# Loading keys and queries already turned, and splitting the weights on TensorE one block per slot

## The chip, the cores and the metric

The kernel runs on one core of one Trainium2 chip. The metric is device time in microseconds of one execution. TensorE is called PE (its weight loads PEld), VectorE DVE, ScalarE ACT, GpSimd POOL, and SyncE, which issues all DMAs here, SP.

## The reference

Top-k attention is followed by a channel mix with a gate. Eight batches, eight heads, 576 tokens, head width 64, model width 512, hidden width 1024. For q, k, v of float32:

```python
scores = scale * np.matmul(q, k.transpose(0, 1, 3, 2))      # per batch and head, 576 x 576
kth = np.partition(scores, -32, axis=-1)[..., -32:-31]       # the 32nd largest of each row
scores = np.where(scores >= kth, scores, -1e9)
attn = exp(scores - max);  attn = attn / (sum(attn) + 1e-9)
x = np.matmul(attn, v), heads side by side                   # batch, 576, 512
x_prev = x shifted by one token
xk = mu_k * x + (1 - mu_k) * x_prev;  xr = mu_r * x + (1 - mu_r) * x_prev
out = sigmoid(xr @ w_r) * (np.maximum(xk @ w_k, 0) ** 2 @ w_v)
```

The three weight matrices arrive as float64 and the mix is computed to more than one fp32r product's precision: each operand is split into a coarse part `hi` and a remainder `lo`, both fp32r, and three products are added (`three`).

## The kernel before

**Slots.** The attention works on tiles of 128 query rows by 576 keys, 288 tiles in all: 8 batches x 4 pairs of heads x 9 tiles. Each batch is visited in eight visits: the four head pairs with tiles 0 to 3 (the first 256 tokens), then the pairs in reverse with tiles 4 to 8 (the other 320). The loop over `n` in `pipeline` is a software pipeline. One turn of it, a slot, issues one step of each of several tiles, in the order written out in `ORDER`. Tile n gets its scores on PE (`score`, L237), which ACT copies to SBUF (`keep`, L246). A slot later DVE takes the eight largest of seven pieces (`c0` to `c6`, L270); in the next slot it sorts out the 24 largest (`best`, `drop`, L273, L276), ACT makes a sign against a bound (`count`, L286), POOL multiplies it with the scores (`below`, L289). In the slot after that, DVE finds the last eight candidates (`eighth`, L915, a line at which the trace puts this MAX8), the threshold (L294) and the masked exponentials (`mask`, L300). Then PE turns them (L313), ACT copies them out (`et`, L317), PE weighs the values (L365), and DVE places the result in `xT` (`place`, L371, L376).

**The mix** runs on PE between the attention's steps, in chunks of mostly 256 tokens (`mix_steps`). A piece is one group of matmuls of about 0.7 us (`PIECE`): a gate step, part of a hidden layer, or one eighth of a value tile. A chunk can begin when its tokens are placed. How many pieces go into a slot is decided by a planner when the program is built (`Lanes`, `work`): each slot credits the lane "pe" with `TENSOR`, never above `CAP`, each attention step charges it (`L.use`), and a piece is issued while the credit covers 0.74 of its cost, at most four a slot. In the last 36 slots a piece is charged 0.56. ACT's and POOL's parts of the mix are placed by similar credits of `PACE` a slot. What is left when the attention ends runs in a tail.

**Keys and queries** lie in DRAM as batch, head, token, d, and PE needs d on the partitions. So SP loads staging tiles (`load_keys`, `load_near`, `load_rest`: tiles `kt`, `q_near`, `qr_in`), PE turns them with an identity (`turn`, L206) into a bank of PSUM, and ACT copies them out to `K` (L214), `qs` (L209) and `qr` (L227) one slot later. The step `prep` does this up to four slots ahead of a visit. Keys of a pair stay in one of four buffers (`KEYS`) for both of its visits in a batch. At the start, `prep_first` and `second` do the first pair at once, with two of the copies on DVE (L221). Each turning is charged 0.35 on "pe" and 0.4 on "act"; the copy of the last 64 queries (`turn_rest`) is not charged.

**Weights.** Twenty blocks of 128x512 float64 numbers are loaded (512 KB each) and split on chip in the first slots, one block in each second slot (`weight_steps` yields twice). The two 32-bit words of a number are treated apart: ACT takes the magnitude of the high word (L126), DVE limits it (L130), shifts it and joins it with the sign to a float32 (L131, L132) and takes its power of two (L140). ACT scales the low word (L136) and copies the value to `hi` as fp32r (L148), POOL subtracts `hi`, multiplies the low word by the power and adds (L149 to L151); for w_v POOL halves the value first (L110). All blocks share one staging area, `early`, so the load of a block waits for the use of the one before. The mix waits for the blocks it needs (`g.ready`).

All four PSUM buffers of the pool `psM` are taken in turn by the turned tiles, the turned keys and queries, the shifted weight bits, and the products of the mix.

Of the kernel before, what the change touches and what calls it, by code (L numbers as in the profile page):

```python
# [21 lines left out]
HS = S // 2  # L22
# [3 lines left out]
KB, KP = 3, 96  # L26
# [19 lines left out]
def topk_attention_channel_mix(ctx: ExitStack, tc: tile.TileContext, q, k, v, mu_k, mu_r, w_k, w_v, w_r, out):  # L46
# [7 lines left out]
    make_identity(nc, ident)  # L54
    ranks_i = consts.tile([128, 9], I32, name="ranks_i")
# [37 lines left out]

    def weight_steps(g, L):

        g.early = g.one.tile([128, HP * (1 + S)], F32, name="early", tag="x1")
# [3 lines left out]
        for src, dst, i, c in blocks:  # L100
            weight_block(g, L, src[i * 128:(i + 1) * 128, c:c + 512], *(d[:, i, c:c + 512] for d in dst), half=dst is wv)
            yield
            yield

    def weight_block(g, L, block, hi, lo, half):
        val = g.early[:, 1024:1536].bitcast(U32)
        valf = val.bitcast(F32)

        def halve():
            nc.gpsimd.tensor_scalar(valf, valf, 0.5, 1.0, op0=OP.mult, op1=OP.mult)  # L110

        if block.dtype == F32:
            nc.sync.dma_start(valf, block)
            if half:
                L.at(1, "pool", halve)
            L.at(2, "act", lambda: nc.scalar.activation(hi, valf, AF.Copy))
            L.at(2, "pool", lambda: g.ready.append(nc.gpsimd.tensor_sub(lo, valf, hi.bitcast(F32))))
            return
        st = g.early[:, :1024].bitcast(U32).rearrange("p (c t) -> p c t", t=2)
        nc.sync.dma_start(g.early[:, :1024].bitcast(U32), block.bitcast(U32))  # L120
        low, high = st[:, :, 0], st[:, :, 1]
        W = Env()

        def magnitude():
            W.mag = g.early[:, 1536:2048].bitcast(U32)
            nc.scalar.activation(W.mag.bitcast(F32), high.bitcast(F32), AF.Abs)  # L126

        def shift():
            bits = g.psM.tile([128, 512], U32, name="wbits", tag="pm")
            nc.vector.tensor_scalar(bits.bitcast(F32), W.mag.bitcast(F32), ZERO, None, op0=OP.max)  # L130
            nc.vector.tensor_scalar(bits, bits, 3, 0x3FFFFFFF, op0=OP.logical_shift_left, op1=OP.bitwise_and)  # L131
            nc.vector.scalar_tensor_tensor(val, high, 0xC0000000, bits, op0=OP.bitwise_and, op1=OP.bitwise_or)  # L132

        def fine():
            W.fine = g.one.tile([128, 512], F32, name="wfine", tag="rest")
            nc.scalar.activation(W.fine, low, AF.Copy, scale=2.0 ** -52)  # L136

        def powers():
            W.exp = g.one.tile([128, 512], U32, name="wexp")
            nc.vector.tensor_scalar(W.exp, val, 0xFF800000, None, op0=OP.bitwise_and)  # L140

        L.at(2, "sign", magnitude)
        L.at(2, "act", fine)
        L.at(2, "dve", shift)
        L.at(3, "dve", powers)
        if half:
            L.at(2, "pool", halve)
        L.at(3, "act", lambda: nc.scalar.activation(hi, valf, AF.Copy))  # L148
        L.at(3, "pool", lambda: nc.gpsimd.tensor_sub(valf, valf, hi.bitcast(F32)))  # L149
        L.at(3, "pool", lambda: nc.gpsimd.tensor_mul(W.fine, W.fine, W.exp.bitcast(F32)))  # L150
        L.at(3, "pool", lambda: g.ready.append(nc.gpsimd.tensor_add(lo, valf, W.fine)))  # L151

# [9 lines left out]
    def load_part(g, x, batch, hp, j, tag=None):  # L162
        t = g.one.tile([128, NKC, 2, D], F32, name="kq", tag=tag or f"kq{j}")
        for i in range(2):
            nc.sync.dma_start(t[:, :, i, :], heads(x, batch, hp)[j, :MAIN].rearrange("(p c) d -> p c d", c=NKC))
        return t

    def load_near(g, x, batch, hp, j, c0):

        t = g.one.tile([128, 2, 2, D], F32, name="q_near", tag=f"kq{j}")  # L170
        for i in range(2):
            nc.sync.dma_start(t[:, :, i, :], heads(x, batch, hp)[j, c0 * 128:(c0 + 2) * 128].rearrange("(c p) d -> p c d", p=128))
        return t

    def load_keys(g, batch, hp, j):
        t = g.one.tile([KP, KB, 2, D], F32, name=f"kt{j}")
        for i in range(2):
            nc.sync.dma_start(t[:, :, i, :], heads(k, batch, hp)[j, i * HS:(i + 1) * HS].rearrange("(b p) d -> p b d", p=KP))
        return t

    def load_rest(g, batch, hp):
        t = g.one.tile([128, 1, 2, D], F32, name="qr_in")
        for j in range(2):
            for i in range(2):
                nc.sync.dma_start(t[j * 64:(j + 1) * 64, 0, i, :], heads(q, batch, hp)[j, MAIN:])
        return t
# [9 lines left out]
    def flat(ap):  # L196
        return ap.rearrange("p e d -> p (e d)")

    def new_k(g, P):
        P.K = g.one.tile([128, 2, HS], F32, name="K", tag=f"K{P.home}")  # L200

    def turn(pt, x):

        n = x.shape[0]
        for c in range(x.shape[1]):
            nc.tensor.transpose(pt[:, c * n:(c + 1) * n], flat(x[:, c]), ident[:n, :n])  # L206

    def copy_out(fast):
        return nc.vector.tensor_copy if fast else lambda to, x: nc.scalar.activation(to, x, AF.Copy)  # L209

    def turn_k(g, P, j, L):
        pt = g.psM.tile([128, MAIN], F32, name="pk", tag="pm")[:, :HS]
        turn(pt, P.kt[j])
        L.at(1, "high", lambda: nc.scalar.activation(P.K[:, j], pt, AF.Copy))  # L214

    def turn_q(g, P, j, L, fast=False):
        n = P.qt[j].shape[1] * 128
        pt = g.psM.tile([128, MAIN], F32, name="pq", tag="pm")[:, :n]
        turn(pt, P.qt[j])
        P.qs[j] = g.one.tile([128, n], F32, name=f"qs{j}")  # L220
        L.at(1, "high", lambda: copy_out(fast)(P.qs[j], pt))  # L221

    def turn_rest(g, P, L):
        pt = g.psM.tile([128, MAIN], F32, name="pr", tag="pm")[:, :128]
        turn(pt, P.rest)
        P.qr = g.two.tile([128, 128], F32, name="qr")
        L.at(1, "high", lambda: nc.scalar.activation(P.qr, pt, AF.Copy))  # L227

# [3 lines left out]
    def scores(g, P, i):  # L232
        hs = [slice(e * 64, (e + 1) * 64) for e in range(2)]
        if i < 2 * NKC:
            c, j = divmod(i - P.first, 2)
            for e, h in enumerate(hs):
                nc.tensor.matmul(g.ps[:, e], lhsT=P.qs[j][h, c * 128:(c + 1) * 128], rhs=P.K[h, j], start=True, stop=True)  # L237
        else:
            for j in range(2):
                for e, h in enumerate(hs):  # L240
                    nc.tensor.matmul(g.ps[hs[j], e], lhsT=P.qr[h, hs[j]], rhs=P.K[h, j], start=True, stop=True)
# [125 lines left out]
    def place(U):  # L367
        xT, hp = U.xT, U.P.hp
        if U.u < 2 and U.P.near:
            x = xT[:, hp, 1 + U.u * 256:1 + (U.u + 1) * 256].rearrange("p (u q) -> p u q", u=2)  # L370
            nc.vector.tensor_mul(x, U.pa, U.ri.rearrange("p (u q) -> p u q", u=2))  # L371
        elif U.u < 2:
            x = xT[:, hp, 1:1 + MAIN].rearrange("p (q c) -> p c q", c=NKC)[:, 2 * U.u:2 * U.u + 2, :]
            nc.vector.tensor_mul(x, U.pa, U.ri.rearrange("p (c q) -> p c q", c=2))
# [264 lines left out]
    def prep_all(g, P, batch, hp, L):  # L639
        P.first, P.near, P.home, P.qs = 0, False, 0, {}  # L640
        new_k(g, P)
        P.rest = load_rest(g, batch, hp)
        P.kt, P.qt = [], []
        load_v(g, P, batch, hp)
        for j in range(2):
            P.kt.append(load_keys(g, batch, hp, j))
            turn_k(g, P, j, L)
            P.qt.append(load_part(g, q, batch, hp, j))
            turn_q(g, P, j, L)
        turn_rest(g, P, L)  # L650

    def prep_first(g, P, batch, hp):

        L = Direct()
        new_k(g, P)
        P.kt = [load_keys(g, batch, hp, 0)]
        P.qt = [load_near(g, q, batch, hp, 0, 0)]
        P.kt.append(load_keys(g, batch, hp, 1))
        P.qt.append(load_near(g, q, batch, hp, 1, 0))
        load_v(g, P, batch, hp)  # L660

        def half(j):
            turn_k(g, P, j, L)
            turn_q(g, P, j, L, True)
        half(0)
        return lambda: half(1)
# [370 lines left out]
```

## Time and profile before

| | |
|---|---|
| median of 3 runs | 1322.38 us (1321.73 to 1330.58) |
| profiled execution, its own time | 1321.01 us |
| span in its trace | 1319.2 us |
| mean granted PE clock | 0.950 |
| DMA | 69.48 MB, mean 53 GB/s |

A row of the groups' view names line, engine, operation, tiles (written <- read), shapes and count; then the busy time in all, the mean duration in ns of one, and the idle time of the engine just before, with what ended it. In the view by windows each row begins with the window and its length; each engine's busy us and count follow, then the granted clock of PE, the DMA share and GB/s. In the list of waits an engine and its line wait for another's line, with the us in total, the times, and the longest. Busy PE counts matmuls that overlap at their ends once.

### The profile page before, as it was taken

To read this page: it belongs to the slowest core of one execution; us is meant where nothing else is said; L and a number is where in the kernel's file an instruction comes from. 1 tells how busy PE (TensorE), PEld (TensorE's weight loads), DVE (VectorE), ACT (ScalarE), POOL (GpSimd) and SP (SyncE) were. 2 spreads that over 40 slices of the span, in tenths; PEclk is the share of its full clock that TensorE was granted. 3 is DMA by queue.
4 is the path that set the end of the run, shared out by engine and by line. 5 is a ranking of instruction groups with operands and counts; after the bars stand their busy time and mean duration, and the time that the engine had idled before them with its cause. 6 is when DMAs were issued, how large, how long until landed. Compare 5 with 4: busy or idle time off the path is not lost.

```text
span 1319.2 us, 34927 instructions
## 1 busy us (share of the span) xinstructions
PE 1181.2 (90%) x11157; PEld 939.8 (71%) x11157; DVE 1128.6 (86%) x6388; ACT 1107.9 (84%) x2716; POOL 907.0 (69%) x837
## 2 busy tenths in 40 slices
PE   5756786899989899799989999999999999999997
PEld 3434564676867688577867787878787787778786
DVE  6999988888998999889998999999999898898100
ACT  5778886889998899898989999999999898898431
POOL 3768887668656866786658776778676758677662
PEclk9766888899999999899989999999999999999999
DMA  4232232211321122112221132122212221111000
GB/s 108 81 93 72 75 94 55 51 33 35 75 63 33 34 63 69 37 37 66 54 58 31 37 75 54 42 55 50 62 43 53 51 59 42 46 40 28 13 17 23
DMA packets 204912, 69.48 MB, mean 53 GB/s; under 512 B 197552, under 2 KB 197552, under 8 KB 204720
## 3 DMA queue, kind: packets, MB, share of 16 engines
q1 hardware_dynamic: 204720, 67.16, 20.4%
q8 instruction: 91, 1.49, 0.5%
q14 instruction: 101, 0.83, 0.2%
HBM read 57.68 MB, written 9.44 MB: 51 GB/s over the span
## 4 chain that ended last, share of the span: by engine, by line
PE 56%; DVE 16%; ACT 15%; POOL 9%; issue 2%; SPq 0%; DMA 0%; ACTq 0%; DVEq 0%; POOLq 0%
PE ps L365 10%; PE ps L237 8%; PE ph L424 5%; PE ph L425 4%; PE ph L426 4%; PE pv L424 4%; PE pt L313 4%; PE pv L426 4%; PE pv L425 3%; DVE cand L270 3%; ACT sc L246 3%; ACT sg L286 3%; DVE E L300 3%; POOL sg L289 3%; DVE top L915 2%; PE pz L424 2%
## 5 line engine op out<-in xcount | busy, mean ns | idle before, releaser
L289 POOL TENSOR_TENSOR sg<-sc,sg 128x576 f32<-128x576 f32 x288 | 410.5, 1425 | 283.2 <-ACT sg L286 277.5
L270 DVE MAX8 cand<-sc 128x8 f32<-128x82 f32 (+1 forms) x2016 | 468.3, 233 | 1.4 <-ACT sc L246 0.9
L915 DVE MAX8 top<-sg 128x8 f32<-128x576 f32 x288 | 217.7, 756 | 40.6 <-POOL sg L289 39.0
L246 ACT ACTIVATE sc<-ps 128x576 f32<-128x576 f32 x288 | 188.9, 656 | 71.2 <-PE ps L237 44.1
L286 ACT ACTIVATE sg<-sc,seen 128x576 f32<-128x576 f32 x288 | 224.5, 780 | 16.1 <-DVE seen L281 14.8
L237 PE MATMUL ps<-K,qs 64*128 64x288 f32 x1024 | 206.8, 483 | 32.8 <-DVE xT L371 15.3
L300 DVE SCALAR_TENSOR_TENSOR E<-sc,seen,se 128x576 f32<-128x576 f32 x288 | 231.8, 805 | 0.6 <-DVE cand L270 0.3
L297 ACT ACTIVATE se<-sc,seen 128x576 f32<-128x576 f32 x288 | 218.7, 759 | 3.6 <-DVE E L300 3.5
L317 ACT ACTIVATE et<-pt 128x320 f32<-128x320 f32 x576 | 219.7, 441 | 0.7 <-PE pt L338 0.7
L313 PEld LDWEIGHTS pt<-ident,E 64*128 64x128 f32 x2880 | 140.8, 145 | 103.6 <-issue 17.1
L365 PE MATMUL ps<-et,v_in 128*64 128x128 f32 (+1 forms) x2560 | 176.4, 285 | 28.1 <-ACT sc L246 19.4
L313 PE MATMUL pt<-ident,E 64*128 64x64 f32 x2880 | 151.2, 232 | 34.2 <-DVE E L300 19.6
L365 PEld LDWEIGHTS ps<-et,v_in 128*64 128x64 f32 x2560 | 146.2, 149 | 48.9 <-ACT sc L246 33.3
L424 PE MATMUL ph<-xh,wk 128*128 128x256 f32 (+2 forms) x608 | 178.9, 294 | 0.4 <-ACT qs L209 0.2
L273 DVE MAX8 top<-cand 128x8 f32<-128x56 f32 x864 | 177.2, 205 | 0.1
L425 PE MATMUL ph<-xl,wk 128*128 128x256 f32 (+2 forms) x608 | 170.8, 281 | 0.0
L426 PE MATMUL ph<-xh,wk 128*128 128x256 f32 (+2 forms) x608 | 170.6, 281 | 0.0
L237 PEld LDWEIGHTS ps<-K,qs 64*128 64x128 f32 x1024 | 81.8, 195 | 81.8 <-ACT sc L246 20.8
L425 PE MATMUL pv<-wv,hh 128*128 128x512 f32 (+1 forms) x296 | 118.1, 399 | 10.7 <-POOL wv L151 10.7
L426 PE MATMUL pv<-wv,hl 128*128 128x512 f32 (+1 forms) x296 | 118.8, 401 | 7.9 <-POOL hl L445 7.9
L424 PE MATMUL pv<-wv,hh 128*128 128x512 f32 (+1 forms) x296 | 125.1, 423 | 0.0
L424 PEld LDWEIGHTS ph<-xh,wk 128*128 128x128 f32 x608 | 116.0, 191 | 5.7 <-ACT qs L209 0.4
(91 smaller groups left out, 2474.9 us busy)
## 6 DMA issues: line engine op xcount, KB each, us to landing
q_near<-in_q SPq DMA_DIRECT2D x256, 64.0 KB, 2.1
v_in<-in_v SPq DMA_DIRECT2D x128, 128.0 KB, 2.5
kt<-in_k SPq DMA_DIRECT2D x128, 72.0 KB, 2.2
out<-eb SPq DMA_DIRECT2D x35, 256.0 KB, 2.1
early<-in_moe_w_k SPq DMA_DIRECT2D x8, 512.0 KB, 3.7
early<-in_moe_w_v SPq DMA_DIRECT2D x8, 512.0 KB, 3.4
vr_in<-in_v SPq DMA_DIRECT2D x64, 32.0 KB, 2.3
early<-in_moe_w_r SPq DMA_DIRECT2D x4, 512.0 KB, 3.5
```

Of the source, the lines that this page charges most:

```text
L237: nc.tensor.matmul(g.ps[:, e], lhsT=P.qs[j][h, c * 128:(c + 1) * 128], rhs=P.K[h, j], start=True, stop=True)
L246: nc.scalar.activation(T.sc.rearrange("p (e k) -> p e k", e=2), T.ps, AF.Copy)
L270: nc.vector.max(T.cand[:, 8 * i:8 * i + 8], T.sc[:, CUTS[i]:CUTS[i + 1]])
L286: nc.scalar.activation(T.side, T.sc, AF.Sign, bias=T.under, scale=-BELOW, accum_out=T.cnt)
L289: nc.gpsimd.tensor_mul(T.side, T.sc, T.side)
L300: nc.vector.scalar_tensor_tensor(T.e, T.sc, T.thr, g.pe, op0=OP.is_ge, op1=OP.mult, accum_out=T.rs)
L313: nc.tensor.transpose(pt[:, c * 64:(c + 1) * 64], T.e[h, k0:k0 + 128], ident[h, h])
L365: nc.tensor.matmul(pa[hs[j]], lhsT=lhsT, rhs=ms[c][j], start=(c == 0), stop=(c == NKC))
L424: nc.tensor.matmul(ps, lhsT=sh, rhs=mh, start=first, stop=False)
L425: nc.tensor.matmul(ps, lhsT=sh, rhs=ml, start=False, stop=False)
L426: nc.tensor.matmul(ps, lhsT=sl, rhs=mh, start=False, stop=last)
L915: nc.vector.max(M.top[:, 24:32], M.side)
```

## The change

Keys and queries are put in the order batch, head, d, token in DRAM before the launch, and go by DMA straight into `K` and `qs`, d on the partitions. All turning of them and its copies go, as do the steps `prep` and `second` and their charges. The staging tiles and `qr` go; `qs` has two buffers and holds all queries of a visit, 256 or 320. Weights go one block per slot through a rotation of staging areas (in the not yet used `hh` and `hl` and in the second `xT`). POOL limits the magnitude and makes `hi`; the remainder is made in PSUM by PE, as value times identity (f32), minus `hi`, and minus the scaled low part (both fp32r), and copied to `lo` by ACT. `TENSOR` goes from 4.10 to 3.90.

```diff
-PACE, TENSOR, SHARE, PIECE, CAP, MOST = 4.60, 4.10, 0.74, 0.71, 4.45, 4
+PACE, TENSOR, SHARE, PIECE, CAP, MOST = 4.60, 3.90, 0.74, 0.71, 4.45, 4
-ORDER = """exp high norm evac best0 c0 drop0 c1 best1 c2 drop1 first score turn inv loads keep sign c3 best2 c4 bounds eighth norm2 count et late below act c5 early thr c6 second mask place mix prep weigh dve pool weights""".split()
+ORDER = """exp wpool high wmul norm evac best0 c0 drop0 c1 best1 c2 drop1 first score turn inv loads keep sign c3 best2 c4 bounds eighth norm2 count et late below act c5 early thr c6 mask place mix weigh wpe dve pool weights""".split()
...
+    unit = consts.tile([128, 2, 128], F32R, name="unit")
+    for i, x in enumerate((-1.0, -2.0)):
+        nc.vector.tensor_scalar(unit[:, i], ident, x, None, op0=OP.mult)
...
+        g.stage = [near[:, :1024], near[:, 1024:], far[:, :1024]]
+        g.mag = [far[:, 1024:1536], far[:, 1536:]]
+        g.val = [early[:, :512], early[:, 512:1024]]
+        g.fine = g.one.tile([128, 512], F32, name="wfine", tag="rest")
+        g.prod = g.one.tile([128, 512], F32R, name="wprod")
+        g.exp = [early[:, 1024:1536], early[:, 1536:2048]]
...
+        for n, (src, dst, i, c) in enumerate(blocks):
+            weight_block(g, L, n, src[i * 128:(i + 1) * 128, c:c + 512], *(d[:, i, c:c + 512] for d in dst), half=dst is wv)
             yield
-            yield
...
+        def coarse():
+            nc.gpsimd.tensor_scalar(hi, valf, scale, 1.0, op0=OP.mult, op1=OP.mult)
+
+        def remains(*more):
+            W.lo = g.psM.tile([128, 512], F32, name="wlo", tag="pm")
+            nc.tensor.matmul(W.lo, lhsT=ident, rhs=valf, start=True, stop=False)
+            for i, x in enumerate(more):
+                nc.tensor.matmul(W.lo, lhsT=x[0], rhs=x[1], start=False, stop=i == len(more) - 1)
+
+        def fine():
+            g.ready.append(nc.scalar.activation(lo, W.lo, AF.Copy, scale=scale))
+
+        L.at(2, "wpool", coarse)
+        L.at(3, "high", fine)
...
         def magnitude():
+            nc.scalar.activation(mag.bitcast(F32), high.bitcast(F32), AF.Abs)
+            nc.gpsimd.tensor_scalar(mag.bitcast(F32), mag.bitcast(F32), ZERO, 1.0, op0=OP.max, op1=OP.mult)
 
         def shift():
             bits = g.psM.tile([128, 512], U32, name="wbits", tag="pm")
+            nc.vector.tensor_scalar(bits, mag, 3, 0x3FFFFFFF, op0=OP.logical_shift_left, op1=OP.bitwise_and)
             nc.vector.scalar_tensor_tensor(val, high, 0xC0000000, bits, op0=OP.bitwise_and, op1=OP.bitwise_or)
+            nc.vector.tensor_scalar(exp, val, 0xFF800000, None, op0=OP.bitwise_and)
+
+        L.at(1, "sign", magnitude)
+        L.at(1, "dve", shift)
+        L.at(2, "high", lambda: nc.scalar.activation(g.fine, low, AF.Copy, scale=-2.0 ** -52))
+        L.at(2, "wmul", lambda: nc.gpsimd.tensor_mul(g.prod, g.fine, exp.bitcast(F32)))
+        L.at(2, "wpe", lambda: remains(less, (unit[:, 0], g.prod)))
...
+    def load_keys(g, P, batch, hp):
+        P.K = g.one.tile([128, 2, HS], F32, name="K", tag=f"K{P.home}")
         for i in range(2):
+            nc.sync.dma_start(P.K[i * 64:(i + 1) * 64], heads(k, batch, hp)[:, :, i * HS:(i + 1) * HS].rearrange("h d s -> d h s"))
+
+    def load_queries(g, P, batch, hp, c0, c1):
+        P.c0 = c0
+        P.qs = g.two.tile([128, 2, c1 - c0], F32, name="qs")
         for i in range(2):
+            nc.sync.dma_start(P.qs[i * 64:(i + 1) * 64], heads(q, batch, hp)[:, :, c0:c1].rearrange("h d s -> d h s"))
...
+                    if N.own and t == (-5 if early else -4):
+                        load_keys(g, N, N.batch, N.hp)
+                    if t == (-4 if early else -3):
+                        load_queries(g, N, N.batch, N.hp, N.c0, N.c1)
...
+        if name in ("q", "k"):
+            a = a.transpose(0, 1, 3, 2)
```

More of the change, by code (lines that the diff above doesn't have):

```diff
@@ L25 @@
 NKC = MAIN // 128
-KB, KP = 3, 96
 HP = H // 2
@@ L94, in weight_steps @@
     def weight_steps(g, L):
-        g.early = g.one.tile([128, HP * (1 + S)], F32, name="early", tag="x1")
+        near = g.one.tile([128, NFB, CH], F32R, name="hh").rearrange("p f n -> p (f n)")
+        far = g.one.tile([128, NFB, CH], F32R, name="hl").rearrange("p f n -> p (f n)")
+        early = g.one.tile([128, HP * (1 + S)], F32, name="early", tag="x1")
+        g.stage = [near[:, :1024], near[:, 1024:], far[:, :1024]]
[4 more added lines that the diff above has]
+        g.exp = [early[:, 1024:1536], early[:, 1536:2048]]
         blocks = [(w_r, wr, i, 0) for i in range(HP)]
@@ L99, in weight_steps, with weight_block @@
         blocks += [(w_v, wv, i, 0) for i in range(NFB)]
-        for src, dst, i, c in blocks:
-            weight_block(g, L, src[i * 128:(i + 1) * 128, c:c + 512], *(d[:, i, c:c + 512] for d in dst), half=dst is wv)
+        for n, (src, dst, i, c) in enumerate(blocks):
+            weight_block(g, L, n, src[i * 128:(i + 1) * 128, c:c + 512], *(d[:, i, c:c + 512] for d in dst), half=dst is wv)
             yield
-            yield
[L105 to L110, printed above, removed]
+    def weight_block(g, L, n, block, hi, lo, half):
+        W = Env()
+        val = g.val[n % 2].bitcast(U32)
+        valf = g.val[n % 2]
+        scale = 0.5 if half else 1.0
+        def coarse():
[9 more added lines that the diff above has]
+        L.at(3, "high", fine)
+        less = unit[:, 1 if half else 0], hi
@@ L112, in weight_block @@
         if block.dtype == F32:
             nc.sync.dma_start(valf, block)
[L114 to L117, printed above, removed]
+            L.at(2, "wpe", lambda: remains(less))
             return
-        st = g.early[:, :1024].bitcast(U32).rearrange("p (c t) -> p c t", t=2)
-        nc.sync.dma_start(g.early[:, :1024].bitcast(U32), block.bitcast(U32))
+        st = g.stage[n % 3].bitcast(U32)
@@ L138, in powers @@
[L138 to L149, printed above, removed]
@@ L175, in load_keys @@
[L175 to L186, printed above, removed]
+            nc.sync.dma_start(P.qs[i * 64:(i + 1) * 64], heads(q, batch, hp)[:, :, c0:c1].rearrange("h d s -> d h s"))
@@ L194, in load_v @@
         nc.sync.dma_start(P.vr[64:], h[:, MAIN:].rearrange("h p d -> p h d"))
[L196 to L227, printed above, removed]
     class Tile_:
@@ L368, in place @@
         xT, hp = U.xT, U.P.hp
[L369 removed]
+        if U.u < 2:
             x = xT[:, hp, 1 + U.u * 256:1 + (U.u + 1) * 256].rearrange("p (u q) -> p u q", u=2)
             nc.vector.tensor_mul(x, U.pa, U.ri.rearrange("p (u q) -> p u q", u=2))
[L372 to L374 removed]
         else:
@@ L637, in spans, with prep @@
         return pieces
[L639 to L643, printed above, removed]
-        load_v(g, P, batch, hp)
[L645 to L666, printed above, removed]
+    def prep(g, P, batch, hp, c0, c1):
+        load_keys(g, P, batch, hp)
+        load_queries(g, P, batch, hp, c0, c1)
+        load_v(g, P, batch, hp)
     def new_batch(g, b=0):
@@ L758, in new_pair @@
             P.b, P.hp, P.part = visits[n]
-            P.first, P.near, P.qs = P.part[0], len(P.part) < 9, {}
+            P.first = P.part[0]
+            P.c0, P.c1 = P.first // 2 * 128, S if 8 in P.part else (P.part[-1] + 1) // 2 * 128
             P.last = n % HP == HP - 1
@@ L775, in pipeline @@
         P = new_pair(0)
-        other = prep_first(g, P, P.batch, P.hp)
+        prep(g, P, P.batch, P.hp, P.c0, P.c1)
         load_mu()
@@ L788, in loads @@
                     early = N.n > 1
-                    if N.own and (t == -5 or t == -4 and not early):
-                        N.kt = [load_keys(g, N.batch, N.hp, 0)]
-                    if t == -4:
-                        N.qt = []
-                        if N.own:
-                            N.kt.append(load_keys(g, N.batch, N.hp, 1))
-                        if 8 in N.part:
-                            N.rest = load_rest(g, N.batch, N.hp)
-                    if t in ((-4, -3) if early else (-3, -2)):
-                        N.qt.append(load_near(g, q, N.batch, N.hp, len(N.qt), N.first // 2))
+                    if N.own and t == (-5 if early else -4):
+                        load_keys(g, N, N.batch, N.hp)
+                    if t == (-4 if early else -3):
+                        load_queries(g, N, N.batch, N.hp, N.c0, N.c1)
                     if t == 5:
@@ L835, in inv @@
                     L.use("act", 0.25)
-            def second():
-                if n == 0:
-                    other()
             def exp():
@@ L850, in weigh_ @@
                         weigh(g, W.U, u)
-            def prep():
-                for N, t in coming(n):
-                    at = (-4, -3) if N.n > 1 else (-3, -2)
-                    if N.own and t == at[0]:
-                        new_k(g, N)
-                    if N.own and t in at:
-                        turn_k(g, N, at.index(t), L)
-                        L.use("pe", 0.35)
-                        L.use("act", 0.4)
-                    if t in (-2, -1):
-                        turn_q(g, N, t + 2, L)
-                        L.use("pe", 0.35)
-                        L.use("act", 0.4)
-                    if t == 0 and 8 in N.part:
-                        turn_rest(g, N, L)
             def norm():
@@ L942, in place_ @@
                     nc.vector.tensor_reduce(least[:, V.P.n // HP:V.P.n // HP + 1], V.P.group[:, :, 1:, o], axis=mybir.AxisListType.XYZ, op=OP.min)
-            do = dict(loads=loads, second=second, score=score, turn=turn_, inv=inv, exp=exp, weigh=weigh_, prep=prep, norm=norm, norm2=norm2, bounds=bounds_,
+            do = dict(loads=loads, score=score, turn=turn_, inv=inv, exp=exp, weigh=weigh_, norm=norm, norm2=norm2, bounds=bounds_,
                       count=count_, below=below_, keep=keep_, mix=mix, eighth=eighth, thr=thr, mask=mask_, place=place_, weights=weights)
@@ L1026 @@
     for name in _INS:
-        a = np.ascontiguousarray(inputs[name])
+        a = np.asarray(inputs[name])
+        if name in ("q", "k"):
+            a = a.transpose(0, 1, 3, 2)
+        a = np.ascontiguousarray(a)
         if a.dtype == np.float64:
```

33 lines of the change are left out of this document (10 added, 23 removed).

## The prediction, made before the change was run

> **What bounds the kernel now.** I read the page first: the engines' totals, the slices, the chain that ended last.
>
> ```profile
> span 1319.2 us, 34927 instructions
> PE 1181.2 (90%) x11157; PEld 939.8 (71%) x11157; DVE 1128.6 (86%) x6388; ACT 1107.9 (84%) x2716; POOL 907.0 (69%) x837
> PEclk9766888899999999899989999999999999999999
> PE 56%; DVE 16%; ACT 15%; POOL 9%; issue 2%; SPq 0%; DMA 0%; ACTq 0%; DVEq 0%; POOLq 0%
> ```
>
> PE is busiest and holds most of the chain, but three engines stand within 6 points of each other, so the average hides stages. The view by windows takes four stretches, and a second one only the clock-throttled part of the first. The columns are busy us of PE, PEld, DVE, ACT and POOL (instructions in brackets), granted clock, DMA share, GB/s.
>
> ```profile
> 0.00:230.00 230.00, 154.64 (x1253) 110.71 (x1253) 203.08 (x993) 174.18 (x402) 163.99 (x147) 0.81 0.31 82
> 230.00:660.00 430.00, 397.67 (x3990) 320.08 (x3987) 398.80 (x2343) 390.20 (x966) 293.18 (x272) 0.97 0.21 50
> 660.00:1210.00 550.00, 529.22 (x5228) 425.99 (x5229) 510.46 (x2993) 504.59 (x1257) 395.23 (x359) 0.99 0.20 49
> 1210.00:1319.20 109.20, 99.65 (x699) 82.98 (x697) 16.31 (x63) 38.89 (x93) 54.58 (x60) 0.97 0.06 19
> 58.00:140.00 82.00, 52.35 (x455) 36.94 (x453) 77.91 (x374) 66.91 (x155) 62.42 (x53) 0.69 0.28 79
> ```
>
> The same windows for the copy of the scores (L246, once per slot) alone give the slots in each; the last row is again 58 to 140 us:
>
> ```profile
> 0.00:230.00 230.00, 27.86 (x44) 0.81 0.31 82
> 230.00:660.00 430.00, 70.64 (x108) 0.97 0.21 50
> 660.00:1210.00 550.00, 89.71 (x136) 0.99 0.20 49
> 58.00:140.00 82.00, 10.27 (x16) 0.69 0.28 79
> ```
>
> So there are four stages. Up to 230 us (weights and first batch) DVE is busy 88%, 95% between 58 and 140 us: DVE-bound. From 230 to 1210 us no engine is full: a slot takes 430/108 = 3.98 and 550/136 = 4.04 us, while DVE works 3.69 and 3.75 us of it, PE 3.68 and 3.89, ACT 3.61 and 3.71. In the tail only PE works, on the channel mix left over.
>
> What keeps DVE from being full is in the list of waits (us in total, times, longest):
>
> ```profile
> POOL sg L289 <- ACT sg L286: 277.5, 176, 14.4
> ACT sc L246 <- PE ps L237: 44.1, 61, 3.5
> DVE top L915 <- POOL sg L289: 39.0, 89, 1.9
> ACT K L214 <- PE pk L206: 14.6, 15, 4.0
> PE pv L425 <- POOL wv L151: 10.7, 3, 3.9
> DVE nmu L92 <- DMA mu<-in_moe_mu_r: 4.1, 1, 4.1
> DVE qs L221 <- PE pq L206: 3.9, 1, 3.9
> ```
>
> DVE's largest wait, the MAX8 at L915, is for POOL, which had itself waited for ACT's sign, and ACT was late behind the score copy or an eviction, which waits for PE. PE's bursts thus travel PE, ACT, POOL, DVE. Relieving PE and ACT helps, but only down to DVE's own 3.69 to 3.75 us a slot.
>
> **The change part by part.**
>
> *Turning goes.* Transposes and their evictions, all forms with over 60 instructions (line, engine, tiles, count, busy us and mean ns, idle before):
>
> ```profile
> L206 PE MATMUL pq<-ident,q_near 128*128 128x128 f32 x256 | 54.3, 296 | 8.9 <-ACT qs L209 5.1 <-DVE early L132 2.1 <-DMA q_near<-in_q 0.6
> L206 PE MATMUL pk<-ident,kt 96*128 96x96 f32 x192 | 29.0, 262 | 4.8 <-DMA kt<-in_k 3.5 <-ACT K L214 1.3
> L209 ACT ACTIVATE qs<-pq 128x256 f32<-128x256 f32 x126 | 49.7, 395 | 9.9 <-PE pq L206 9.0
> L214 ACT ACTIVATE K<-pk 128x288 f32<-128x288 f32 x64 | 26.6, 416 | 15.9 <-PE pk L206 14.6
> ```
>
> L206 alone, by windows (PE, then PEld), and the landing time of a key load:
>
> ```profile
> 230.00:660.00 430.00, 31.74 (x178) 21.46 (x178) 0.97 0.21 50
> 660.00:1210.00 550.00, 38.59 (x214) 26.47 (x214) 0.99 0.20 49
> ```
>
> ```profile
> kt<-in_k SPq DMA_DIRECT2D x128, 72.0 KB, 2.2
> ```
>
> PE loses 0.29 and 0.28 us a slot, to 3.39 and 3.61. ACT loses at least (49.7 + 26.6)/288 = 0.26, to 3.35 and 3.45. DVE loses nothing and becomes the bound, by 0.30 us a slot over PE in the second stage and by 0.14 in the third. The new loads are fewer and issue no later than the old ones; SP's queue loses the small q and rest transfers. A key buffer is written by DMA where ACT wrote it before, but it was last read three visits earlier, and the two query buffers are free a visit ahead. I cost the loads at nothing, hidden behind four slots of lead; a lead lost would cost one DMA landing, 2.2 us, per visit.
>
> How full does DVE get? The nearest row is 58 to 140 us, where it was the bound at 95%, with weight waits in it; 99% is the most I allow. I take 97%: 3.69/0.97 = 3.80 and 3.75/0.97 = 3.87 us a slot. Stage two: 108 x 3.80 = 411 (before 430). Stage three: 136 x 3.87 = 526 (before 550). At 95% they are 420 and 537, at 99% 403 and 515.
>
> *Weights.* Rows of the old steps, per block of 128x512, and of the nearest operations to the new ones:
>
> ```profile
> L131 DVE TENSOR_SCALAR wbits<-wbits 128x512 uint32<-128x512 uint32 x20 | 14.0, 700 | 0.7
> L140 DVE TENSOR_SCALAR wexp<-early 128x512 uint32<-128x512 uint32 x20 | 13.9, 697 | 0.0
> L130 DVE TENSOR_SCALAR wbits<-early 128x512 f32<-128x512 f32 x20 | 13.8, 690 | 6.1 <-ACT et L317 3.5 <-ACT ri L344 1.9 <-ACT early L126 0.8
> L132 DVE SCALAR_TENSOR_TENSOR early<-early,wbits 128x512 uint32<-128x512 uint32 x20 | 13.8, 689 | 2.1 <-POOL wk L151 0.4
> L136 ACT ACTIVATE wfine<-early 128x512 f32<-128x512 uint32 x20 | 13.5, 677 | 10.3 <-POOL wk L151 4.3 <-POOL wv L151 3.1 <-POOL wr L151 2.8
> L126 ACT ACTIVATE early<-early 128x512 f32<-128x512 f32 x20 | 13.4, 671 | 0.0
> L150 POOL TENSOR_TENSOR wfine<-wfine,wexp 128x512 f32<-128x512 f32 x20 | 25.5, 1276 | 0.0
> L441 ACT ACTIVATE r<-ph 128x512 f32<-128x512 f32 x64 | 38.2, 597 | 8.7 <-PE ph L426 8.7
> L110 POOL TENSOR_SCALAR early<-early 128x512 f32<-128x512 f32 x8 | 4.9, 618 | 3.2 <-DVE early L132 3.2
> L148 ACT ACTIVATE wk<-early 128x512 fp32r<-128x512 f32 x8 | 5.0, 628 | 0.0
> L289 POOL TENSOR_TENSOR sg<-sc,sg 128x576 f32<-128x576 f32 x288 | 410.5, 1425 | 283.2 <-ACT sg L286 277.5
> L237 PE MATMUL ps<-K,qs 64*128 64x288 f32 x1024 | 206.8, 483 | 32.8 <-DVE xT L371 15.3
> L425 PE MATMUL pv<-wv,hh 128*128 128x512 f32 (+1 forms) x296 | 118.1, 399 | 10.7 <-POOL wv L151 10.7
> ```
>
> DVE's maximum (L130) moves to POOL: minus 13.8 us on the bound. The other three stay, 2.09 us a block, but now in each of 20 slots and not in each second one. In 58 to 140 us DVE worked 77.91/16 = 4.87 us a slot with half a block (2.78/2 = 1.39) in it, so attention is 3.48, and a slot with a whole new block is 5.57. Do the others stay below? ACT: 66.91/16 = 4.18, less half the old three steps (L126, L136, L148: 1.98/2 = 0.99), plus new 0.671 + 0.677 + 0.597 = 1.95: 5.15, less the copies gone. POOL: sign product (L289) 1.43, maximum and coarse part 2 x 0.618, product 1.276: 3.9. PE: 3.27 a slot at clock 0.69, plus the remainder: one f32 product of 512 columns and two fp32r. No row shows this f32 shape. Nearest above is the score product (L237), 64x288 in 483 ns, two records for each product in the code, so at most 2 x 483 x 512/288 = 1.72 us; below, two passes of the 0.399 of L425, whose operands are fp32r. With two fp32r products at about 0.4 the block is 1.6 to 2.5 us; I take 2.0, and PE is at 5.3. PE and ACT end just under DVE, so nothing is added in the forecast; if both spill, I price it at 1 us for each of 20 slots.
>
> All weights are there near slot 23, not 42, so the stall of PE for the weights (10.7 us, three times) goes, and what follows the first chunk is done sooner. DVE's first work came behind the wait for mu and a query copy (4.1 and 3.9 us): with seven DMAs ahead of mu instead of eleven and no copy, I take 4 us less. Stage one: 203 busy less 14, plus idle of 27 less 4 (start) less 4 (stalls): 208. Bounds: 203 with idle down to 14, 219 with half the gain.
>
> *Planner.* TENSOR falls from 4.10 to 3.90, but the charge of 0.35 for each of 192 turnings (0.233 a slot) goes too. Charged per slot besides: 0.92 + 0.47 + 0.70 = 2.09. So (4.10 - 2.09 - 0.233)/0.71 = 2.50 pieces of mix a slot before and 2.55 after. Until about batch 4 the mix waits for tokens, not budget; over the last 136 slots this makes some 6 pieces fewer in the tail, at 0.7 us minus 4, a bit more since the cap of 4.45 no longer cuts. Tail: 109 to 104; bounds 100 and 109.
>
> *Sum:* 208 + 411 + 526 + 104 = 1249, plus 4 of reserve for the half spill of the weights: 1253. The profiled execution took 1321.01 us with a span of 1319.2, so 1255; the median of the runs shown, 1322.38, lies 1.4 above it: **1256 us**.
>
> **The rivals.**
> 1. *DVE nearly full* (99%): 203 + 403 + 515 + 100 = 1221, so 1224. For it: in early slots it idles only 5%, weights included. Against: ACT stays at 88% and comes in bursts.
> 2. *Half the gain.* DVE stays at 95%, ACT's bursts still reach L915 through POOL: 219 + 420 + 537 + 107 = 1283, so 1286. For it: L915's waits never name PE directly.
> 3. *No change to measure:* the weight slots spill (plus 20) and the third stage stays as it is, because PE at 3.61 of 3.75 still blocks: 228 + 420 + 550 + 109 = 1307, so 1310.
> 4. *Slower: the clock.* With the turnings gone PE has gaps in slots without mix, and if the clock drops in stage two to the 0.69 of 58 to 140 us, PE needs 3.39 x 0.97/0.69 = 4.77 us a slot: 515 for 411, in all 1360. It decides where the saving is eaten up: 66 us over 108 slots is 4.41 a slot, a clock of 0.75. [...] Against the rival: half clock sits where PE did only attention and turning (0.69), and 230 to 1210 us has 0.97 to 0.99 because of the mix, which stays at the same pieces per slot.
>
> That the change doesn't do what it says is no rival: the turnings are simply not issued.
>
> **How the numbers follow.** Forecast 0.60, nearly full 0.13, half gain 0.17, no change 0.05, clock 0.05. The range reaches from 1224 (rival 1's time) to 1288 (rival 2 and the 95% bound). Below lie half of rival 1, above rivals 3 and 4 and a bit of rival 2: about 0.2. One per cent, 13 us, is about what a measurement of this kernel can tell from no change. Faster by more: 0.91; within: 0.05; slower: 0.04.
>
> **What would show it.** No L206, qs, K or qr copies. The score copies' pitch from batch 1 on at 3.8 to 3.87 us with DVE at 96 to 98% and PE near 90% and 94%. The first 44 score copies within 208 us, weight slots near 5.6, clock in them above 0.69 if the remainder counts as work. The waits of L915 for POOL about halved. A tail of 104 us. I am wrong if DVE waits on as before (ACT was the cause), if weight slots pass 6.5 us, or if the clock falls after 230 us.

## The result, and the profile after

The changed kernel takes 1279.89 us (median of four runs, 1278.86 to 1281.25), against 1326.48 for the kernel before on the same chip: a ratio of 0.965, 95% interval 0.9604 to 0.9696. The forecast was 1256, the range 1224 to 1288. The profiled execution took 1280.38 us with a span of 1278.5. This is device time: putting keys and queries in the new order before the launch is not in it. The kernel before sat now near 1322 and now near 1333 us within one set of runs, which is why ratios have wide intervals; sizes of stages below are taken from the profiled spans, 1319.2 before and 1278.5 after, 40.7 us apart.

The page of the changed kernel (span; engines; clock in 40 slices; the chain by engine):

```profile
span 1278.5 us, 33370 instructions
PE 1149.8 (90%) x10757; PEld 893.0 (70%) x10757; DVE 1107.6 (87%) x6368; ACT 1043.6 (82%) x2494; POOL 903.1 (71%) x829
PEclk8787899998989899799999999999999998999999
PE 49%; DVE 22%; ACT 14%; POOL 11%; issue 2%; SPq 1%; DMA 0%; ACTq 0%; DVEq 0%; POOLq 0%
```

PE lost 31 us of busy time and ACT 64, DVE 21, POOL 4. PE's share of the chain fell from 56 to 49%, DVE's rose from 16 to 22%: the bound has moved towards DVE, but not over to it. The view by windows, cut at nearly the same slots as before (the columns are those explained above):

```profile
0.00:214.00 214.00, 162.47 (x1260) 105.80 (x1260) 185.90 (x965) 161.62 (x365) 162.12 (x139) 0.87 0.31 90
214.00:638.00 424.00, 383.12 (x3783) 303.29 (x3784) 397.32 (x2349) 366.57 (x884) 291.35 (x272) 0.94 0.19 50
638.00:1171.00 533.00, 505.27 (x5028) 401.01 (x5027) 508.49 (x2998) 476.47 (x1156) 395.26 (x360) 0.99 0.19 50
1171.00:1278.50 107.50, 98.94 (x691) 82.91 (x689) 15.90 (x60) 38.89 (x93) 54.34 (x60) 0.97 0.06 19
```

The copy of the scores (now L202) in the first three of them:

```profile
0.00:214.00 214.00, 28.45 (x44) 0.87 0.31 90
214.00:638.00 424.00, 70.22 (x108) 0.94 0.19 50
638.00:1171.00 533.00, 89.78 (x137) 0.99 0.19 50
```

So the four stages went from 230 to 214, from 430 to 424, from 550 to 533 and from 109 to 107.5 us. In the second stage a slot still takes 424/108 = 3.93 us, with DVE at 94% (93% before), and the clock fell from 0.97 to 0.94; in the third 533/137 = 3.89, DVE at 95% (93% before).

Lines from the list of waits, of the whole run (engine and line, what it waited for, us in total, times, longest):

```profile
POOL sg L245 <- ACT sg L242: 251.2, 154, 4.4
...
ACT sc L202 <- PE ps L192: 54.7, 65, 5.1
...
DVE top L819 <- POOL sg L245: 29.1, 72, 0.8
...
DVE wbits L151 <- POOL hl L147: 12.1, 18, 5.2
...
DVE nmu L94 <- DMA mu<-in_moe_mu_r: 6.6, 1, 6.6
```

DVE waits less for the sign product (39.0 to 29.1 us), and the waits for turned keys and queries are gone. One line is worse than thought: a new wait of 12.1 us for the limited magnitude (L147), 5.2 of it once at the start. The wait for mu is 6.6 us against 4.1, but it begins earlier, as DVE no longer waits 3.9 us for a query copy first: DVE's first MAX8 starts at 8.44 us, where it started at 10.15.

### The profile page after: what moved, and what is told of

Same layout as the page of the kernel before. It is cut to its first block, busy times and chain, and to the rows that moved or that the text cites. A ratio compares the mean times of both kernels' runs of the same rounds, so it can differ in the third digit from the quotient of the medians.

```text
span 1278.5 us, 33370 instructions
## 1 busy us (share of the span) xinstructions
PE 1149.8 (90%) x10757; PEld 893.0 (70%) x10757; DVE 1107.6 (87%) x6368; ACT 1043.6 (82%) x2494; POOL 903.1 (71%) x829
## 4 chain that ended last, share of the span: by engine, by line
PE 49%; DVE 22%; ACT 14%; POOL 11%; issue 2%; SPq 1%; DMA 0%; ACTq 0%; DVEq 0%; POOLq 0%
PE ps L321 10%; PE ps L192 7%; DVE cand L226 5%; DVE top L819 4%; POOL sg L245 4%; DVE E L256 4%; ACT sc L202 4%; PE pv L377 4%; PE pv L379 3%; PE pt L269 3%; PE ph L377 3%; PE pv L378 3%; PE ph L378 3%; PE ph L379 3%; ACT sg L242 3%; PE pz L377 2%
## 5 line engine op out<-in xcount | busy, mean ns | idle before, releaser
L202 ACT ACTIVATE sc<-ps 128x576 f32<-128x576 f32 x288 | 188.8, 656 | 120.7 <-PE ps L192 54.7
L819 DVE MAX8 top<-sg 128x8 f32<-128x576 f32 x288 | 217.2, 754 | 31.2 <-POOL sg L245 29.1
L192 PE MATMUL ps<-K,qs 64*128 64x288 f32 x1024 | 202.6, 472 | 32.7 <-ACT sc L202 16.2
L321 PE MATMUL ps<-et,v_in 128*64 128x128 f32 (+1 forms) x2560 | 177.0, 286 | 44.1 <-ACT sc L202 39.6
L269 PEld LDWEIGHTS pt<-ident,E 64*128 64x128 f32 x2880 | 135.6, 142 | 76.4 <-issue 19.7
L269 PE MATMUL pt<-ident,E 64*128 64x64 f32 x2880 | 143.5, 227 | 14.1 <-DVE top L229 10.6
```

Of the source, the lines that this page charges most:

```text
L192: nc.tensor.matmul(g.ps[:, e], lhsT=P.qs[h, j, x:x + 128], rhs=P.K[h, j], start=True, stop=True)
L202: nc.scalar.activation(T.sc.rearrange("p (e k) -> p e k", e=2), T.ps, AF.Copy)
L269: nc.tensor.transpose(pt[:, c * 64:(c + 1) * 64], T.e[h, k0:k0 + 128], ident[h, h])
L321: nc.tensor.matmul(pa[hs[j]], lhsT=lhsT, rhs=ms[c][j], start=(c == 0), stop=(c == NKC))
L819: nc.vector.max(M.top[:, 24:32], M.side)
```

## The experiments

Below, "slots 22 to 44" and the like run from one score copy to another, in the profiled execution of the run. Time from the start to the 45th copy, slots 54 to 150, slots 150 to 287 and the tail: before 233.5, 381.2, 551.1, 109.2; after 217.6, 379.0, 533.9, 107.8. (The ten slots between, 44 to 54, took 44.1 and 40.2.) The records of the granted clock know two values here, full and half; "half clock" is the time spent at half.

**Each part alone.** First the changed kernel with the old `weight_steps` and `weight_block`:

```diff
-    (new weight_steps, weight_block: one block a slot)
+    (old weight_steps, weight_block: a block in each second slot)
```

> The turning part of the change alone (with TENSOR at 3.90); weights in the old way, a block in each second slot. Theory, the two parts add and the turnings carry the gain after the first batch: the stretch from the 44th score copy to the last, 980 us before and 957 after the whole change, is 957 here too, and the first stretch gains some 4 us of start alone, so about 1294 us, ratio about 0.978. Rival, the weights carry most (early weights let the mix start sooner): at most 10 us gained, 1312 or more, ratio 0.99 or above.

Measured: 1290.09 us (ratio 0.9685, 0.9636 to 0.9734). The stages are 230.5, 373.2, 535.5 and 108.0. Then the kernel before with the new weights alone, its turnings and TENSOR of 4.10 kept:

```diff
-    (old weight_steps, weight_block)
+    (new weight_steps, weight_block, unit; wpool, wmul, wpe in ORDER)
```

> The weight part alone; keys and queries still turned on chip, TENSOR 4.10. Theory: only the stretch up to the 44th score copy changes, 230 to about 218 us, and the rest keeps its 980 and 109 us: about 1309 us, ratio about 0.990. Rival, early weights carry most: 1295 or less, ratio below 0.98.

Measured: 1308.89 us (ratio 0.9836, 0.9787 to 0.9885), stages 218.5, 382.0, 550.7 and 109.5. The theory held for both in time and in stages; the ratios are lower than expected because the kernel before measured 1332.8 us beside these two. In spans, the turnings alone give 30.4 us, the weights 16.0, both together 40.7. The weights act almost only before the 45th copy, the turnings almost only behind it. Six us are lost where they meet, most of them in slots 54 to 150: 373.2 us with the turnings alone, 379.0 with both.

**Is DVE the bound?** One MAX8 more in each slot, in both kernels:

```diff
                 if C:
                     f(C, r)
+                    if f is best and r == 0:
+                        f(C, r)
```

> The changed kernel with the first MAX8 of the sorting (128x56, 205 ns alone, 122 ns from its start to the next instruction's) issued twice in each slot, result unchanged: 288 x 0.12 to 0.205 us, 35 to 59 us more work on DVE. Theory, DVE is now the bound: the time rises by 0.8 or more of that, 30 to 50 us over the changed kernel. Rival, the bound is still a chain through PE and ACT: it rises by less than 15 us.

> The kernel before with the same extra MAX8. Theory, DVE was not the bound between 230 and 1210 us, PE's bursts were: the time rises by clearly less than in the changed kernel, 10 to 25 us. Rival, DVE bound it before as well: as much as in the changed kernel, 30 to 50 us.

Measured: 1309.85 us for the changed kernel (30.0 more), 1349.78 for the kernel before (17.0 more by the medians, 27.9 by the spans; the granted clock was 0.932 in this profile and 0.950 in that of the kernel before). DVE's busy time rose by 55.6 and 57.5 us. So of each us of DVE work about 0.54 reaches the end now: at the lower edge of the theory's 30 to 50 us and below its 0.8. Before, it was 0.30 by the medians, as the theory for the kernel before had it, and 0.49 by the spans. The windows of slots 54 to 150 and 150 to 287 in the lengthened changed kernel:

```profile
261.10:649.10 388.00, 346.06 (x3402) 271.32 (x3398) 373.93 (x2194) 330.25 (x789) 257.05 (x243) 0.93 0.18 49
649.10:1200.10 551.00, 513.93 (x5033) 406.39 (x5030) 536.35 (x3142) 481.69 (x1157) 395.98 (x361) 0.98 0.18 49
```

The first grew by 9.0 us (379.0 to 388.0), the second by 17.1, and DVE came to 96 and 97%. In the kernel before, the same slots grew by 14.2 and 9.8, but half clock rose there too, from 13.7 to 41.0 and from 13.7 to 27.3 us, so how firm DVE's hold on each stage was before can't be read from this pair. What holds DVE up in the changed kernel between slots 54 and 287, first lines of DVE's own waits:

```profile
DVE top L819 <- POOL sg L245: 25.2, 61, 0.8
DVE rs L283 <- ACT rs L279: 6.0, 10, 0.7
DVE xT L327 <- ACT sc L202: 4.9, 5, 1.5
DVE nine L250 <- ACT se L253: 4.4, 9, 0.9
```

Half of the 49 us that DVE idles there is still the wait for POOL's sign product, the end of the chain PE, ACT, POOL, DVE.

**Is PE still on the path?** Four extra products in slots behind one without a piece of mix:

```diff
+        for _ in range(fill):
+            nc.tensor.matmul(g.pt[0], lhsT=unit[:, 0], rhs=wk[0][:, 0, :512], start=True, stop=True)
...
-                    turn_tile(g, V, L)
+                    turn_tile(g, V, L, 4 if n > 44 and not state.get("did") else 0)
```

> The changed kernel with four fp32r products of 512 columns (some 0.23 us each, into a bank that the next transposes overwrite) before the turning in every slot that follows a slot without a piece of mix, from slot 45 on. They add work to PE and nothing else. Theory, half clock in the slots without mix (48 us of slots 54 to 150, against 14 before) keeps the second stage at 379 us: the half clock there falls below 20 us and the stage to about 371, so about 1272 us in all. Rival, the chain through the shared bank and ACT sets the stage and the clock doesn't matter: the stage stays at 379 or grows by the products, 1280 to 1290.

Measured: 1324.55 us. Half clock in slots 54 to 150 did fall, from 47.8 to 10.2 us, but the products cost more than it gave: PE's busy time rose by 63.8 us (1149.8 to 1213.6 on the page) and the time by 44.7, so 0.70 of each us. Most slots without mix are those that weigh values, and the slot behind them is where PE has to catch up, as I read it. PE remains on the path there, with 90% of the whole span busy. As a test of the clock this one is spoilt. The next puts the products only where PE has time, within slots 54 to 149:

```diff
-                    turn_tile(g, V, L)
+                    turn_tile(g, V, L, 4 if 54 <= n < 150 and not state.get("did") and not last and not (tiles.get(n - 6) and ends(tiles[n - 6])) else 0)
```

> As the run with fillers, but only in slots 54 to 149 that follow a slot without mix, and not in or behind a slot that weighs values, so that PE has spare time where they stand. Theory, half clock in the empty stretches costs the second stage some 6 us: half clock in slots 54 to 150 falls from 48 to about 20 us, the stage from 379 to about 373, 1274 us in all. Rival, the clock's dips lie where PE has time to spare and cost nothing: the stage stays within 2 us of 379 although the half clock falls.

Measured: 1278.84 us, the stage 375.8, half clock 27.3 us. Slots 54 to 150 of the changed kernel, of the one with these few products, and of the one with the turnings gone alone:

```profile
257.80:636.70 378.90, 344.14 (x3400) 271.26 (x3398) 354.57 (x2098) 325.87 (x788) 257.19 (x243) 0.94 0.19 51
```

```profile
258.00:633.80 375.80, 341.28 (x3419) 268.02 (x3416) 354.77 (x2098) 326.51 (x788) 257.21 (x243) 0.96 0.19 51
```

```profile
272.10:645.20 373.10, 340.38 (x3454) 268.35 (x3452) 353.90 (x2096) 328.67 (x792) 262.42 (x247) 0.98 0.19 51
```

The granted clock goes 0.94, 0.96, 0.98, half clock 47.8, 27.3, 13.7 us, the stage 379, 376, 373; DVE does the same work in all three. That is the theory's order and half its size in the second. But four other runs (below) had 34 to 38 us of half clock and the stage at 376 with no such products, so the products themselves bought nothing that shows, and the whole time of this run is 1 us from the changed kernel's, which is no difference.

Those other runs settle more. The one that leaves out POOL's limit differs from the changed kernel only in the weights' steps, which end by slot 23. Up to copy 96 (counted from 0, as the slots are) it keeps step with the changed kernel, to 0.4 us over slots 54 to 96 and to 0.01 over the last six of them. Then half clock strikes in one of them and not in the other. Copies 96 to 98 and 117 to 126 by windows, first in the changed kernel, then without the limit:

```profile
423.30:434.10 10.80, 10.09 (x102) 7.95 (x102) 9.01 (x50) 6.08 (x18) 7.59 (x7) 0.70 0.00 0
504.70:543.80 39.10, 31.67 (x264) 23.43 (x260) 34.65 (x206) 31.76 (x75) 24.51 (x21) 0.78 0.18 46
```

```profile
417.80:427.50 9.70, 7.70 (x102) 5.80 (x102) 9.02 (x50) 6.04 (x18) 7.49 (x7) 1.00 0.00 0
498.10:535.40 37.30, 29.62 (x264) 22.21 (x260) 34.53 (x206) 32.01 (x76) 24.54 (x21) 0.82 0.19 48
```

DVE, ACT and POOL do the same work; the clock and PE's time differ, and the first half clock begins 0.4 us before copy 96, ahead of any lateness. These two places and a third behind copy 133 cost 3.3 us; less the 0.3 by which the changed kernel was ahead, that is the 3.0 us between 379.0 and 376.0. The last run below repeats the changed kernel's clock and its 379 (51.2 us of half clock), two others repeat 376. So 3 of the 6 us are the clock's. The other 3, between 376 and 373, stay open: there the mix comes in another order. By the 55th copy 270 matmuls of the mix have begun in the changed kernel, 216 with the old weights and 234 with the new weights alone, so here the mix gets ahead of its tokens; then four slots in a row have no piece (62 to 65), where each of the other two has at most three.

**What else could hold DVE at 94 to 95%?** The sums of the values in a buffer of their own:

```diff
-            U.pa = g.sums[U.u // 2]
+            t = g.psM.tile([128, 512], F32, name="pa", tag="pm")
+            U.pa = t[:, :256].rearrange("p (u q) -> p u q", u=2) if U.u < 2 else t[:, :64]
```

> The changed kernel with the weighed sums in a buffer of the rotation of four, not in the banks of the scores. Theory, PE's 96 us of waits (weigh behind the copy of the scores) are mostly hidden: within 5 us of 1280. Rival, this coupling is what keeps DVE at 94 to 95% in slots 54 to 287: DVE goes to 97%, 20 us less, 1260. A loss is possible too, as the rotation has one more taker.

Measured: 1290.27 us, ten more, though it was 5 us ahead at the 45th copy (212.5 for 217.6). The weighing no longer waits for the score copy, but for the placing, and ACT's wait for scores doubled; from its list of waits:

```profile
ACT sc L202 <- PE ps L192: 109.1, 101, 5.1
...
DVE top L820 <- POOL sg L245: 43.4, 93, 1.4
...
PEld pa L322 <- DVE xT L328: 19.5, 18, 3.1
```

The four buffers in rotation seem to be the scarcer thing, so this neither confirms the coupling nor clears it: taking one for the sums costs more behind the weight slots. And less mix work for ACT and POOL in a slot:

```diff
-PACE, TENSOR, SHARE, PIECE, CAP, MOST = 4.60, 3.90, 0.74, 0.71, 4.45, 4
+PACE, TENSOR, SHARE, PIECE, CAP, MOST = 3.90, 3.90, 0.74, 0.71, 4.45, 4
```

> The changed kernel with the credit of ACT and POOL lowered from 4.60 to 3.90 a slot, so that fewer of the mix's parts are put into one slot. Theory, ACT's remaining lateness comes from waiting for PE's scores, not from too much work in a slot: within 5 us of 1280. Rival, bursts of ACT and POOL keep DVE at 94 to 95%: DVE at 97%, 1265 or less.

Measured: 1284.86 us, slots 150 to 287 in 541.4 instead of 533.9, DVE at 94% there. Spreading the planned mix work thinner gives DVE no more room; bursts of another origin are not excluded by it.

**The weight slots.** POOL without the maximum, then DVE with it:

```diff
-            nc.gpsimd.tensor_scalar(..., ZERO, 1.0, op0=OP.max, op1=OP.mult)
+            nc.gpsimd.tensor_scalar(..., 1.0, 1.0, op0=OP.mult, op1=OP.mult)
```

> The changed kernel with POOL multiplying the magnitude by one instead of limiting it to 2^-15 from below; this leaves out the limit on tiny weights. Theory, the maximum on POOL (1915 ns against 618 for a multiplication of the same shape) makes POOL the bound of the weight slots: DVE's 12 us of waits for it go and the first 44 slots end 10 us earlier, about 1270 us. Rival, DVE is the bound there at 5.57 us a slot as predicted and the wait only moves elsewhere: within 3 us of 1280.

```diff
-            nc.gpsimd.tensor_scalar(..., ZERO, 1.0, op0=OP.max, op1=OP.mult)
...
+            nc.vector.tensor_scalar(bits.bitcast(F32), mag.bitcast(F32), ZERO, None, op0=OP.max)
```

> The changed kernel with the maximum back on DVE (690 ns a block). Theory: DVE pays 20 x 0.69 = 13.8 us and saves the 12 us of waiting for POOL, so within 4 us of 1280. Rival, the prediction's own term, that the move took 14 us off the bound: 1292 or more.

Measured: 1272.40 and 1284.60 us; the first 22 slots 123.5 and 134.4, where the changed kernel has 131.3. The first is near the theory; the second is just beyond the theory's 4 us and far below the rival's 1292. Both profiles also have the 376 us of slots 54 to 150, the clock's 3 us less, so the effect of the maximum is better read from the first slots than from the whole. POOL's step in the changed kernel and with the maximum left out:

```profile
L147 POOL TENSOR_SCALAR hl<-hl 128x512 f32<-128x512 f32 x20 | 38.3, 1916 | 11.3 <-ACT hl L146 11.3
```

```profile
L147 POOL TENSOR_SCALAR hl<-hl 128x512 f32<-128x512 f32 x20 | 12.3, 614 | 12.4 <-ACT hl L146 12.4
```

Same engine, shape and types: with the maximum the step took 1916 ns, with a multiplication in its place 614. The maximum is what binds the weight slots, as POOL's timeline of one of them shows (start, length):

```profile
67.40 0.85 POOL L121 TENSOR_SCALAR wk<-early 128x512 fp32r<-128x512 f32 x1 [0.21 <-DVE early L152]
68.22 1.27 POOL L158 TENSOR_TENSOR wprod<-wfine,early 128x512 fp32r<-128x512 f32 x1
69.45 1.92 POOL L147 TENSOR_SCALAR hl<-hl 128x512 f32<-128x512 f32 x1
71.34 0.41 POOL L288 TENSOR_SCALAR rb<-rs 128x256 f32<-128x256 f32 x1
71.71 1.41 POOL L245 TENSOR_TENSOR sg<-sc,sg 128x576 f32<-128x576 f32 x1
73.09 0.79 POOL L121 TENSOR_SCALAR wk<-early 128x512 fp32r<-128x512 f32 x1
```

and DVE's of the same time:

```profile
71.41 0.69 DVE L151 TENSOR_SCALAR wbits<-hl 128x512 uint32<-128x512 uint32 x1 [0.17 <-POOL hl L147]
72.19 0.69 DVE L152 SCALAR_TENSOR_TENSOR early<-hh,wbits 128x512 uint32<-128x512 uint32 x1
```

POOL is busy from one block to the next (0.85 + 1.27 + 1.92 + 0.41 + 1.41 in 5.7 us; the records overlap a little at their ends). One turn of this, from one L153 to the next, by windows:

```profile
67.34:72.91 5.57, 4.81 (x20) 2.00 (x20) 5.27 (x25) 4.51 (x11) 5.51 (x5) 0.69 0.39 131
```

POOL has 5.51 of 5.57 us, DVE 5.27. And it is a ring as well: coarse part, product, maximum, then DVE's two steps, whose value the next coarse part needs. Two tries to take the coarse part out of it follow.

```diff
-            nc.gpsimd.tensor_scalar(hi, valf, scale, 1.0, op0=OP.mult, op1=OP.mult)
+            nc.scalar.activation(hi, valf, AF.Copy, scale=scale)
...
-        L.at(2, "wpool", coarse)
+        L.at(2, "high", coarse)
```

> The changed kernel with the coarse part of the weights made by ACT (638 ns in the kernel before) and no longer by POOL (840 ns), which keeps the maximum of 1915 ns. Theory, POOL bounds the weight slots: it falls by 0.84 us a block, more than the 0.65 us that DVE waits, so the first 22 slots take about 123 us as in the run without the limit, and the whole about 1272 us. Rival, ACT becomes the bound of the weight slots: within 3 us of 1280 or above.

Measured: 1291.15 us, first 22 slots 143.7. The rival's "or above" covers the time but not its reason: ACT is busy 70% of these slots, as in the changed kernel. From its waits between 10 and 130 us:

```profile
POOL wprod L158 <- ACT wfine L157: 26.9, 13, 4.4
DVE wbits L151 <- POOL hl L147: 22.1, 18, 6.6
```

On ACT's queue the coarse part stands ahead of the low word (L157) and waits for DVE's value (15 times between 10 and 130 us, 16.2 us in all); so the low word comes late, POOL's product waits for it, and the maximum and DVE behind that. The ring had become longer, not shorter. Put behind the copy of the scores, ACT's coarse part stands ahead of neither:

```diff
-        L.at(2, "high", coarse)
+        L.at(2, "sign", coarse)
```

> As the run with the coarse part on ACT, but behind the copy of the scores, where ACT does not hold up the scaled low word that POOL waits for. Theory, the weight slot of 5.57 us is a ring of POOL's coarse part, product and maximum and two steps of DVE; with 0.85 us out of it and nothing put in its place, DVE sets the slot at about 5.3 us as in the run without the limit: first 22 slots 123 to 126 us, 1272 to 1275 us in all. Rival, ACT's added 0.63 us a slot shows up in any place: 1280 or more.

Measured: 1280.64 us (1278.84 to 1282.02), first 22 slots 128.3. These slots are shorter by 3 us instead of 5 to 8, and the whole is the same as the changed kernel. ACT is then busy 79% of these slots instead of 70%; what took the rest back stays open. No version that keeps all of the computation was measurably faster than the changed kernel.

## Why the prediction was right, and which sizes were off

The direction was right, and so was most of the mechanism: the turnings gave most of the gain, through PE and ACT down towards DVE's own work; no stage became slower, and behind the first slots no wait in the list names the new loads. The time lay in the range, but the gain was 46.6 us by the medians where some 66 were forecast, and the 1279.89 us are nearer to rival 2's 1286 than to the forecast's 1256. Term by term rival 2 (219, 420, 537, 107) is the nearer one as well, against 214, 424, 533 and 107.5 measured, and its condition came true: DVE stayed near 95%, and its largest wait ahead of the tail is still for POOL's sign product, down from 39.0 to 29.1 us where "about halved" was said. By the prediction's terms:

- *Stage one,* 208 forecast, 214 measured. DVE's work fell by 17 us where 14 were forecast (the last section has the rest). The idle time did not fall, 27 before and 28 after. The term "maximum 0.618" took a multiplication's row for a maximum: it is 1.916, so POOL needs 5.5 us a block instead of 3.9 and DVE waits for it. The coarse part took 0.84, not 0.618, as well. The max_dve run puts the worth of the move at 3 to 5 us, not 14. The forecast 5.57 us for a weight slot came out in the slot shown (5.9 on average over slots 4 to 21), but by luck: POOL's ring sets it, while DVE's sum, from which it was worked out, is 5.27. The start gave 1.7 us (DVE's first MAX8 at 8.44 for 10.15), not 4.
- *Stage two,* 411 forecast, 424 measured. The failed step is "I take 97%": DVE came only from 93 to 94%. With the turnings gone alone it came to 95% in slots 54 to 150 (353.90 of 373.1), so some 6 us go to the meeting of both parts, 3 of them by the clock. The rest I put down to two engines sharing the path in turn, which a mean of 90% on PE hides: 0.54 of added DVE work and 0.70 of the PE work added behind slots without mix reach the end. No run takes this sharing away, so that it is what keeps DVE from 97% is argued, not shown.
- *Stage three,* 526 forecast, 533 measured, by the same step: 95.4% for 97%.
- *Tail,* 104 forecast, 107.8 measured. The step that more credit leaves fewer pieces was wrong. The first matmul of each group of three, after the last score copy, before and after:

```profile
1210.00:1319.20 109.20, 61.57 (x188) 34.68 (x188) 0.97 0.06 19
```

```profile
1170.70:1278.50 107.80, 61.54 (x188) 34.76 (x188) 0.97 0.06 19
```

  188 in both, and in every other run here too, with either `TENSOR`: the same work is left, whatever the credit. That the placing of the last tokens sets its amount is my reading.
- *The clock,* rival 4, came true in small: 0.97 to 0.94 in the second stage, not 0.69, at a price of 3 us shown and 6 at most. In the weight slots the clock rose (0.82 to 0.87 up to the 45th copy). That comes with PE's products for the remainder: 0.89 with the new weights alone, 0.79 with the turnings gone alone. Taking the turnings out went with 0.82 to 0.79 and 0.89 to 0.87, but moved other work as well, so what the turnings themselves do to the clock was not shown.
- *PE's and ACT's loads* in the weight slots were judged well enough: PE was busy 4.81 us and ACT 4.51 of the 5.57 us shown, so neither bound them.

## What to carry to other kernels

With two engines each busy some 90%, taking work off one gave less here than the distance to the other's sum. So double a small piece of work on each, and see how much of it reaches the end, before counting on 97%. When two runs of nearly the same program differ by a few us, lay their slots side by side: here that found the clock's 3 us. Price a step that moves to another engine by that engine's row for the same operation, not only the same shape. And before moving an operation within an engine's queue, look at what stands behind it: the same copy on ACT cost 11 us in one place and nothing in another.

## What the runs showed of the hardware

- On POOL, a tensor-scalar step with a maximum took 1916 ns for 128x512 f32, with two multiplications 614 ns.
- The f32 product of 512 columns (L125) shows as two records of 813 ns on average, 592 to 1223, at a mean granted clock of 0.83 in the first 131 us; the upper bound taken, 859 each, was near that average.
- DVE's power-of-two step got cheaper by the order alone. Its line before and after, in the view of one line (shortest, median and longest ns, first and last start):

```profile
L140 DVE TENSOR_SCALAR wexp<-early x20: 417/660/1166, 20.6 to 219.3; 128x512 uint32<-128x512 uint32 x20
```

```profile
L153 DVE TENSOR_SCALAR early<-early x20: 426/426/496, 16.2 to 125.7; 128x512 uint32<-128x512 uint32 x20
```

  Before, it took 417 to 428 ns where POOL ran nothing at its start or was about to end, and otherwise it ended some 285 ns behind POOL's running step, mostly a sign product: 847 with 562 ns of that left, 1166 with 881, 470 with 186. In the changed order it comes before POOL's coarse part, which needs a value of DVE's, and meets the end of a sign product only four times (486 to 496 ns). This is 5 us of DVE's 17 in stage one that the prediction did not have. The trace of the changed kernel shows the other side too: POOL's coarse part (L121), begun while L153 ran, ended 475 to 481 ns behind it in all 20 blocks, whether it began 0.05 or 0.17 to 0.19 us after it.
